# Loading x in 1 KB packets, with a column permutation on TensorE's output side

## The chip, the cores and the metric

One Trainium2 chip, one of its cores. The metric is the device time of the slowest core in microseconds (us); here there is one core, so it is that core's time.

## The reference

The kernel runs a cross attention between x (8 batches, 8 heads, 512 rows of 64) and a small state (32 rows per head), joins both read-outs to 544 rows of 512, applies a two-dimensional Fourier transform, and then a normalised two-layer MLP with a residual.

```python
scores  = x @ state^T / 8;   a  = softmax(scores);   xread = a  @ state   # 512 rows
scores2 = state @ x^T / 8;   a2 = softmax(scores2);  sread = a2 @ x       # 32 rows
X = concat(xread, sread)                     # (8, 544, 512) after joining the heads
u = X + real(fft(fft(X, axis=1), axis=2))
out = u + relu(layernorm(u) @ w_ch1) @ w_ch2 # w_ch1: 512 x 2048, w_ch2: 2048 x 512
```

## The kernel before

One row of x per partition; each packet of a load is one row of one head, 64 fp32 values, 256 B. The Fourier transform wants the 512 rows in an order in which rows 0 to 287 rise and the rest are mirrored. With one row per partition that order costs nothing: whole tiles are multiplied by an identity or by a mirror matrix and land in adjacent columns of PSUM.

```python
def load_x(b):                                  # six loads per batch, packets of 256 B
    xb = x[b].rearrange("h s d -> s h d")
    for n, (ps, si, rows) in enumerate(( (slice(32, 128), 2, xb[288:384]), (slice(0, 128), 0, xb[1:129]), ... )):
        queue = nc.scalar if b == 0 and n in (1, 3) else nc.sync
        queue.dma_start(out=xs[ps, si, :].rearrange("p (h d) -> p h d", d=D), in_=rows)

load_state(0, 1); load_x(0); load_state(1, 2); load_x(1)
nc.sync.dma_start(out=s_dram[2:]..., in_=state[2:, :, ::-1, :]...)   # states 2..7, first hop, to DRAM
load_state(2, B, s_dram)                                             # second hop, to SBUF

def more_loads():                               # GpSimd, in this order
    nc.gpsimd.tensor_copy(gate[:, 0:1], XQs[0][:, 3, 0, 0:1])
    cast_x(1); clears(1)
    nc.gpsimd.memset(stb[:, 2:]..., 0.0)

def last_loads():
    for hh in range(1, 4): low_tables(hh)       # reads the scratch that becomes the hidden layer's buffer
    nc.gpsimd.tensor_tensor(gate, xs_of[0][:, :, 0], w1[:, :, 3 * 512], op=ALU.add)   # waits for w1
    load_x(2)
    nc.gpsimd.tensor_copy(gate[:, 0:1], xs_of[2][:, 0, 0:1])                          # waits for x of batch 2
    for q in range(4): nc.gpsimd.dma_start(out=w2[:, q * 4:(q + 1) * 4, :], in_=...)  # fp32 read, bf16 written
    state_blocks(2, 3, nc.gpsimd.tensor_copy)   # waits for the states
    cast_x(2)

def turn_scores(g):                             # batches 2 to 7, two groups each
    p = qt("eTp")                               # a PSUM bank, 512 fp32 columns
    for si, o, rhs in ((0, 0, ident), (1, 128, ident), (2, 256, ident[:, 0:32]),
                       (2, 416, mirror[:, 0:96]), (3, 288, mirror)):
        nc.tensor.matmul(p[:, o:o + rhs.shape[1]], lhsT=E[:, si, g, :], rhs=rhs, start=True, stop=True)
    nc.scalar.activation(ET[:, g, :], p, AF.Copy, accum_out=sums[:, g:g + 1])
```

GpSimd works through its queue in order, so what stands behind a waiting instruction waits too. After `cast_x(2)` come the folds of batch 1 (tiles XE, XO, Sm), which VectorE (XQ) and then TensorE (gp) need. In the profiles ph and po are the matmuls of the MLP's first and second layer, gp and yp those of the transform, xT is x transposed, hT the hidden layer, eTp a group of scores, XR, XF and XL the read-outs, XE, XO and Sm GpSimd's folds.

The softmax here doesn't subtract the row's maximum and nothing guards it: scores larger than these inputs give would overflow.

## Time and profile before

| | before |
|---|---|
| time, median of 3 | 314.31 us (314.26 to 314.36) |
| span of the profiled run | 312.3 us |
| TensorE busy, 0 to 28.64 us (to the first MLP matmul) | 21.8 of 28.6 us |
| TensorE busy, 28.64 us to the end | 276.1 of 283.7 us |
| DMA packets, of them under 512 B | 114292, 105688 |
| a turned score group (5 matmuls, 512 columns) | 0.23 us |
| second hop of the states issued, used by GpSimd | 26.2 us, 35.8 us |

SyncE's wait for the first hop (engine and line, what was waited for, us, times, longest), and what GpSimd waited for before it could issue w1:

```profile
SPq L108 <- DMA s_dram<-in_state_dram: 14.1, 1, 14.1
10.14 0.19 POOL L274 COPY gate<-gen 128x4 f32<-128x4 f32 x1 [0.47 <-DVE gen L203]
```

A line in the order of time begins with its start and its length in us, then the engine, the line of the source and what is written and read; a bracket tells how long the engine had been idle and what ended it. In a chain of waits the columns are start, length, engine, tile and source line; "issue" there is time in which the profile shows nothing waited for.

### The profile page before, as it was taken

To read this page: it belongs to the slowest core of one execution; us is meant where nothing else is said; L and a number is where in the kernel's file an instruction comes from. 1 tells how busy PE (TensorE), PEld (TensorE's weight loads), DVE (VectorE), ACT (ScalarE), POOL (GpSimd) and SP (SyncE) were. 2 spreads that over 40 slices of the span, in tenths; PEclk is the share of its full clock that TensorE was granted. 3 is DMA by queue.
4 is the path that set the end of the run, shared out by engine and by line. 5 is a ranking of instruction groups with operands and counts; after the bars stand their busy time and mean duration, and the time that the engine had idled before them with its cause. 6 is when DMAs were issued, how large, how long until landed. Compare 5 with 4: busy or idle time off the path is not lost.

```text
span 312.3 us, 5918 instructions
## 1 busy us (share of the span) xinstructions
PE 297.9 (95%) x2268; PEld 171.3 (55%) x2300; DVE 184.9 (59%) x442; ACT 137.7 (44%) x269; POOL 74.8 (24%) x171
## 2 busy tenths in 40 slices
PE   5878999999999999999999999999999999999995
PEld 5666997544554545456645554455445544455443
DVE  8695882877778484864727774686559563100112
ACT  7698764635533543333542444234433432333300
POOL 8758884410240040300500024002200131000000
PEclk9999999999999999999999999999999999999999
DMA  9999999268354925268333684531333037303047
GB/s 158 187 200 180 173 181 186 59 113 180 61 109 85 201 65 136 67 129 160 80 80 78 144 177 95 126 84 52 80 75 68 34 76 99 79 36 67 34 105 166
DMA packets 114292, 34.86 MB, mean 112 GB/s; under 512 B 105688, under 2 KB 110040, under 8 KB 114264
## 3 DMA queue, kind: packets, MB, share of 16 engines
q1 hardware_dynamic: 103544, 28.72, 46.2%
q0 software_dynamic: 4224, 4.19, 8.6%
q10 hardware_dynamic: 6496, 1.57, 2.5%
q8 instruction: 18, 0.29, 0.4%
q14 instruction: 10, 0.08, 0.1%
HBM read 22.41 MB, written 14.02 MB: 117 GB/s over the span
## 4 chain that ended last, share of the span: by engine, by line
PE 79%; DVE 13%; ACT 2%; DMA 2%; issue 2%; SPq 0%; POOL 0%; DVEq 0%; POOLq 0%; ACTq 0%
PE po L768 32%; PE ph L703 29%; PE gp L578 4%; PE ph L713 3%; DMA xs<-in_x_dram 2%; DVE U L548 2%; DVE st L318 2%; PE po L760 1%; PE yp L544 1%; PE xfp L436 1%; PE xrp L436 1%; PE yp L543 1%; PE gp L582 1%; PE esp L411 1%; DVE XF L445 1%
## 5 line engine op out<-in xcount | busy, mean ns | idle before, releaser
L768 PE MATMUL po<-w,hT 128*128 128x512 bf16 x476 | 122.0, 379 | 1.5 <-issue 0.8
L705 ACT ACTIVATE hT<-ph 128x512 bf16<-128x512 f32 x112 | 66.9, 597 | 124.8 <-PE ph L703 124.8
L703 PE MATMUL ph<-unT,w 128*128 128x512 bf16 x437 | 114.0, 379 | 1.0 <-DVE ot L734 0.3
L703 PEld LDWEIGHTS <-w 128*128 128x128 bf16 x576 | 51.1, 98 | 47.9 <-issue 0.8
L768 PEld LDWEIGHTS <-hT 128*128 128x128 bf16 x496 | 47.1, 98 | 45.3
L734 DVE SCALAR_TENSOR_TENSOR ot<-po,rstd,U 128x512 f32<-128x512 f32 (+2 forms) x33 | 24.2, 732 | 52.8 <-PE po L768 44.9
L588 POOL COPY GL<-G 128x128 bf16<-128x128 bf16 x8 | 2.3, 291 | 113.6 <-ACT G L586 113.6
L548 DVE TENSOR_TENSOR U<-yp,XR 128x512 f32<-128x512 f32 x16 | 10.9, 683 | 27.0 <-PE yp L544 27.0
L318 DVE BATCH_NORM_STATS2 st<-U 128x6 f32<-128x512 f32 x32 | 21.8, 682 | 0.1
L324 POOL TENSOR_TENSOR rstd<-mv,epst 128x1 f32<-128x1 f32 x34 | 6.8, 200 | 62.9 <-DVE mv L320 62.9
L325 POOL TENSOR_TENSOR rstd<-rstd,mhalf 128x1 f32<-128x1 f32 x34 | 20.9, 615 | 2.7
L788 PE MATMUL warm<-ident 128*128 128x128 bf16 x152 | 13.5, 246 | 3.7 <-POOL ident masks.py:199 3.4
L586 ACT CAST G<-gp 128x288 bf16<-128x288 f32 x31 | 12.0, 397 | 10.7 <-PE gp L582 5.7
L713 PE MATMUL ph<-unT,w 128*128 128x128 bf16 x256 | 16.1, 219 | 0.5 <-ACT unT L624 0.5
L713 PEld LDWEIGHTS <-w 128*128 128x128 bf16 x256 | 15.0, 98 | 0.8 <-issue 0.6
L788 PEld LDWEIGHTS <-ident 128*128 128x128 bf16 x152 | 11.8, 113 | 4.7 <-POOL ident masks.py:199 3.4
L578 PEld LDWEIGHTS <-XQ 128*128 128x128 bf16 x96 | 8.8, 98 | 8.9 <-DVE XQ L508 2.6
L138 POOL CAST xin<-xs 128x2048 bf16<-128x2048 f32 x7 | 13.2, 1888 | 0.1
L612 DVE TENSOR_SCALAR ub<-U,mv 128x512 bf16<-128x512 f32 x24 | 12.3, 511 | 1.1 <-DVE mv L320 0.3
L436 PEld LDWEIGHTS <-ET 128*128 128x128 bf16 x80 | 7.0, 98 | 9.5 <-DVE XF L445 1.8
L445 DVE TENSOR_TENSOR XR<-xrp,rs 128x512 bf16<-128x512 f32 x16 | 11.1, 695 | 1.3 <-POOL XR L278 0.7
L715 ACT ACTIVATE hT<-ph 128x512 bf16<-128x512 f32 x16 | 9.4, 598 | 3.9 <-PE ph L713 3.9
(191 smaller groups left out, 350.4 us busy)
## 6 DMA issues: line engine op xcount, KB each, us to landing
xs<-in_x_dram SPq DMA_DIRECT2D x22, 256.0 KB, 5.0
w<-in_moe_w_ch_dram POOLq DMA_DIRECT2D x8, 512.0 KB, 10.4
out_dram<-ot SPq DMA_DIRECT2D x15, 256.0 KB, 2.5
r_dram<-ot SPq DMA_DIRECT2D x14, 256.0 KB, 2.0
out_dram<-r_dram SPq DMA_DIRECT2D x14, 256.0 KB, 3.6
xs<-in_x_dram SPq DMA_DIRECT2D x8, 192.0 KB, 4.5
xs<-in_x_dram ACTq DMA_DIRECT2D x2, 256.0 KB, 4.2
l_dram<-ot SPq DMA_DIRECT2D x2, 256.0 KB
```

The lines of the kernel that those rows point to most:

```text
L318: nc.vector.bn_stats(st6, u)
L325: nc.gpsimd.tensor_tensor(rstd, rstd, mhalf, op=ALU.pow)
L436: nc.tensor.matmul(ph[:, 0:260], lhsT=ET[:, g, c0:c0 + 128], rhs=rhs, start=True, stop=True)
L445: nc.vector.tensor_tensor(ov, in0=p[ps, :, 0:256].rearrange("p g (h d) -> p g h d", d=D), in1=rs[ps].unsqueeze(3).to_broadcast([n, 2, 4, D ...
L548: nc.vector.tensor_add(u.rearrange("p (k r) -> p k r", r=2), p.rearrange("p (r k) -> p k r", r=2)[:, 0:u.shape[1] // 2, :], x.rearrange("p ...
L578: nc.tensor.matmul(p[:, 0:NM], lhsT=XQ[:, j, c, :], rhs=tab[c], start=(c == 0), stop=(c == 2 and j != 2))
L703: nc.tensor.matmul(ph[:, o:o + n], lhsT=w1[:, c, f * 128:(f + 1) * 128], rhs=un_of[key][:, c, :], start=(c == 0), stop=(c == DC - 1))
L705: nc.scalar.activation(hT[:, per * i:per * i + per, :].rearrange("p a b -> p (a b)"), ph, AF.Relu, scale=-1.0 if key in flipped else 1.0)
L713: nc.tensor.matmul(ph[:, o:o + 128], lhsT=w1[:, c, f * 128:(f + 1) * 128], rhs=un_of[key][:, c, 128 * r:128 * r + 128], start=(c == 0), st ...
L734: nc.vector.scalar_tensor_tensor(ot[:, cols], in0=po_of[i][:, 0:cols.stop - cols.start], scalar=rstd, in1=u[:, cols], op0=ALU.mult, op1=AL ...
L768: nc.tensor.matmul(po_of[i], lhsT=h_of[key][:, f, i * 128:(i + 1) * 128], rhs=w2[:, f, :], start=(f == 0), stop=(f == FC - 1))
L788: nc.tensor.matmul(t[:, 0:128], lhsT=ident, rhs=ident, start=(i == 0), stop=(i == n - 1))
```

## The change

Its intent: fewer and larger packets for x, so that batch 0 lands sooner. Four consecutive rows of a head lie together in memory (1 KB), so a partition takes rows 4p to 4p + 3. The rows of x then lie four apart in the tiles, and the order that the transform needs is restored by the matmul that writes the scores: its output columns have a step of four. With it go fewer VectorE steps for the arguments of the sine tables, and a new order on several queues; the load of states 2 to 7 goes from behind batch 1's x to behind batch 2's.

```diff
     def load_x(b):
+        xb = x[b].rearrange("h (p i) d -> p h (i d)", i=4)
+        n = 2 if b == 0 else 4
+        for h in range(0, H, n):
+            queue.dma_start(out=xs[:, h:h + n, :], in_=xb[:, h:h + n, :])
     ...
-    nc.sync.dma_start(out=s_dram[2:]..., in_=state[2:, :, ::-1, :]...)
-    load_state(2, B, s_dram)
+    def load_more_state():                     # the same two hops, called later
     ...
-    state_blocks(0, 1)                         # ScalarE
-    nc.scalar.activation(CL..., zeros, AF.Copy)
-    nc.scalar.activation(SL..., zeros, AF.Copy)
+    state_blocks(0, 1, nc.gpsimd.tensor_copy)
-    nc.gpsimd.tensor_copy(gate, q2_[:, 0:4])   # GpSimd waited here for VectorE's second table
     for q in range(4): nc.gpsimd.dma_start(out=w1..., in_=...)
+    nc.gpsimd.memset(CL..., 0.0)
+    nc.gpsimd.memset(SL..., 0.0)
     clears(0)
+    state_blocks(1, 2, nc.gpsimd.tensor_copy)
     def more_loads():
         cast_x(1)
+        nc.gpsimd.tensor_tensor(gate, xs_of[0][:, 0:4, 0], w1[:, :, 3 * 512], op=ALU.add)
+        load_x(2)
+        load_more_state()
         clears(1)
         nc.gpsimd.memset(stb[:, 2:]..., 0.0)
     def last_loads():
-        nc.gpsimd.tensor_tensor(gate, xs_of[0][:, :, 0], w1[:, :, 3 * 512], op=ALU.add)
-        load_x(2)
     ...
     def scores_t(g):                           # batches 0 and 1: 4 matmuls become 18
-        for lo, hi, src in ((0, NM, slice(0, NM)), (NM, S, slice(S - 1, NM - 1, -1))):
+        for i in range(4):
+            x0 = 128 * i
+            for cols, rows in ((slice((i - 1) % 4, 285 if i == 0 else 288, 4), slice(x0 + (i == 0), x0 + 72)),
+                               (slice(287, 288), slice(0, 1)) if i == 0 else (None, None),
+                               (slice(291 - i, S, 4), slice(x0 + 127, x0 + 71, -1))):
     def turn_scores(g):                        # batches 2 to 7: 5 matmuls become 8
+            for si in range(4):
+                for o, rhs in (((3, ident[:, 1:72]), (287, mirror[:, 0:57])) if si == 0 else
+                               ((si - 1, ident[:, 0:72]), (291 - si, mirror[:, 1:57]))):
+                    nc.tensor.matmul(p[:, o:o + 4 * rhs.shape[1] - 3:4], lhsT=E[:, si, g, :], rhs=rhs, ...)
     ...                                        # cut: table arguments in fewer VectorE steps, constants, low rows
-    warm(48)
+    warm(12)
```

More of the change, by code (lines that the diff above doesn't have):

```diff
@@ L72 @@
     li = gen2[:, 3072:3072 + 384].bitcast(I32)
-    nc.gpsimd.iota(lt[:, 0:256], pattern=[[1, 256]], base=1, channel_multiplier=0)
-    nc.gpsimd.iota(lt[:, 256:NM], pattern=[[1, NL]], base=256, channel_multiplier=0)
+    nc.gpsimd.iota(lt, pattern=[[1, NM]], base=1, channel_multiplier=0)
     nc.gpsimd.iota(pi_[:, 0:2], pattern=[[128, 2]], base=1, channel_multiplier=1)
@@ L78 @@
     for hh in range(4):
-        nc.gpsimd.iota(pi_[32 * hh:32 * hh + 32, 2:3], pattern=[[0, 1]], base=256, channel_multiplier=1)
+        nc.gpsimd.iota(pi_[32 * hh:32 * hh + 32, 2:3], pattern=[[0, 1]], base=257, channel_multiplier=1)
     nc.gpsimd.iota(li[:, 0:128], pattern=[[2, 128]], base=1, channel_multiplier=0)
@@ L84, with more_constants @@
     mirror = singles.tile([128, 128], BF16, name="mirror")
-    nc.gpsimd.memset(halfpi, PI / 2)
-    nc.gpsimd.memset(mhalfpi, -PI / 2)
-    nc.gpsimd.memset(epst, eps)
-    nc.gpsimd.memset(mhalf, -0.5)
-    nc.gpsimd.memset(mirror, 0.0)
-    nc.gpsimd.affine_select(out=mirror, in_=mirror, compare_op=ALU.not_equal, fill=1.0, base=-127,
-                            pattern=[[1, 128]], channel_multiplier=1)
-    sg = singles.tile([128, 5], F32, name="sg")
-    nc.gpsimd.tensor_copy(sg[:, 0:1], pi_[:, 3:4])
-    nc.gpsimd.tensor_scalar(sg[:, 1:2], in0=sg[:, 0:1], scalar1=0.5, scalar2=-0.25, op0=ALU.mult, op1=ALU.add)
-    nc.gpsimd.tensor_scalar(sg[:, 1:2], in0=sg[:, 1:2], scalar1=float(1 << 23), scalar2=None, op0=ALU.add)
-    nc.gpsimd.tensor_scalar(sg[:, 1:2], in0=sg[:, 1:2], scalar1=float(1 << 23), scalar2=4.0, op0=ALU.subtract, op1=ALU.mult)
-    nc.gpsimd.tensor_scalar(sg[:, 0:1], in0=sg[:, 0:1], scalar1=-2.0, scalar2=1.0, op0=ALU.mult, op1=ALU.add)
-    nc.gpsimd.tensor_add(sg[:, 0:1], sg[:, 0:1], sg[:, 1:2])
-    turn_w = 2.0 * PI / 512 * (1.0 - 1e-6)
-    nc.gpsimd.tensor_scalar(sg[:, 2:3], in0=sg[:, 0:1], scalar1=PI / 2, scalar2=None, op0=ALU.mult)
-    nc.gpsimd.tensor_scalar(sg[:, 3:4], in0=sg[:, 0:1], scalar1=-turn_w, scalar2=None, op0=ALU.mult)
+    halves = ((halfpi, PI / 2), (mhalfpi, -PI / 2), (epst, eps), (mhalf, -0.5))
+    sg = singles.tile([128, 5], F32, name="sg")
+    sgi = singles.tile([128, 1], I32, name="sgi")
+    def more_constants():
+        for t, v in halves:
+            nc.gpsimd.memset(t, v)
+        nc.gpsimd.memset(mirror, 0.0)
+        for base in (-128, 0):
+            nc.gpsimd.affine_select(out=mirror, in_=mirror, compare_op=ALU.not_equal, fill=1.0, base=base,
+                                    pattern=[[1, 128]], channel_multiplier=1)
     stf = gen2[:, 1024:2048].rearrange("p (b g d) -> p b g d", b=B, g=2)
@@ L116, in load_x, with cast_x @@
     def load_x(b):
-        xs = wk.tile([128, 4, dm], F32, name="xs", tag="xs")
-        xb = x[b].rearrange("h s d -> s h d")
-        for n, (ps, si, rows) in enumerate((
-            (slice(32, 128), 2, xb[288:384]),
-            (slice(0, 128), 0, xb[1:129]),
-            (slice(0, 128), 1, xb[129:257]),
-            (slice(0, 128), 3, xb[384:512]),
-            (slice(2, 32), 2, xb[258:288]),
-            (slice(0, 2), 2, xb[0:258:257]),
-        )):
-            queue = nc.scalar if b == 0 and n in (1, 3) else nc.sync
-            queue.dma_start(out=xs[ps, si, :].rearrange("p (h d) -> p h d", d=D), in_=rows)
-        xs_of[b] = xs
-    def cast_x(b):
-        xs, t = xs_of[b], xin_bufs[b % 2]
-        if b == 0:
-            for si in (0, 3, 1):
-                nc.scalar.copy(t[:, si, 1:513], xs[:, si, :])
-            nc.gpsimd.tensor_copy(t[:, 2, 1:513], xs[:, 2, :])
-        else:
-            nc.gpsimd.tensor_copy(t[:, :, 1:513], xs)
+        xs = wk.tile([128, H, 4 * D], F32, name="xs", tag="xs")
+        xb = x[b].rearrange("h (p i) d -> p h (i d)", i=4)
+        n = 2 if b == 0 else 4
+        for h in range(0, H, n):
+            queue = nc.scalar if b == 0 and h in (0, 4) else nc.sync
+            queue.dma_start(out=xs[:, h:h + n, :], in_=xb[:, h:h + n, :])
+        xs_of[b] = xs
+    def cast_x(b, copy=nc.gpsimd.tensor_copy, lo=0, hi=H):
+        copy(xin_bufs[b % 2][:, :, 1 + D * lo:1 + D * hi].rearrange("p i (h d) -> p h i d", d=D),
+             xs_of[b][:, lo:hi, :].rearrange("p h (i d) -> p h i d", d=D))
     load_state(0, 1)
@@ L143 @@
     load_x(1)
-    nc.sync.dma_start(out=s_dram[2:].rearrange("b h j d -> (b h) j d"),
-                      in_=state[2:, :, ::-1, :].rearrange("b h j d -> (b h) j d"))
-    load_state(2, B, s_dram)
+    def load_more_state():
+        nc.sync.dma_start(out=s_dram[2:].rearrange("b h j d -> (b h) j d"),
+                          in_=state[2:, :, ::-1, :].rearrange("b h j d -> (b h) j d"))
+        load_state(2, B, s_dram)
     for i in range(2):
@@ L169 @@
     state_ones(0, 2)
-    state_blocks(0, 1)
+    state_blocks(0, 1, nc.gpsimd.tensor_copy)
+    more_constants()
     CL = singles.tile([128, 4, NM], BF16, name="CL")
     SL = singles.tile([128, 4, NM], BF16, name="SL")
-    zeros = gate2[:, 0:1].to_broadcast([128, 4 * NM])
-    nc.scalar.activation(CL.rearrange("p a b -> p (a b)"), zeros, AF.Copy)
-    nc.scalar.activation(SL.rearrange("p a b -> p (a b)"), zeros, AF.Copy)
-    cast_x(0)
+    cast_x(0, nc.scalar.copy, 0, 2)
+    cast_x(0, nc.scalar.copy, 2, 4)
+    cast_x(0, lo=4, hi=6)
     w1 = singles.tile([128, DC, dff], BF16, name="w1")
@@ L202, in absolute, with turn @@
     def absolute(q, f):
-        nc.vector.scalar_tensor_tensor(q, in0=f, scalar=-1.0, in1=f, op0=ALU.mult, op1=ALU.max)
-    def turn(W, N, lf, cols, scratch, eng=nc.vector):
+        nc.vector.tensor_scalar(q.bitcast(I32), in0=f.bitcast(I32), scalar1=0x7fffffff, scalar2=None, op0=ALU.bitwise_and)
+    def turn(W, N, lf, cols, scratch):
         n = len(cols)
-        f = scratch[:, 0:n * W].rearrange("p (n w) -> p n w", w=W)
-        q = scratch[:, n * W:2 * n * W].rearrange("p (n w) -> p n w", w=W)
+        f2d, q2d = scratch[:, 0:n * W], scratch[:, n * W:2 * n * W]
+        f, q = [t.rearrange("p (n w) -> p n w", w=W) for t in (f2d, q2d)]
@@ L209, in turn @@
         for i, c in enumerate(cols):
-            eng.tensor_scalar(f[:, i, :], in0=lf, scalar1=pf[:, c:c + 1], scalar2=None, op0=ALU.mult)
-        eng.tensor_scalar(q, in0=f, scalar1=1.0 / N, scalar2=float(1 << 23), op0=ALU.mult, op1=ALU.add)
-        eng.tensor_scalar(q, in0=q, scalar1=float(1 << 23), scalar2=-float(N), op0=ALU.subtract, op1=ALU.mult)
-        eng.tensor_add(f, f, q)
-        if eng is nc.vector:
-            absolute(q, f)
+            nc.vector.tensor_scalar(q[:, i, :], in0=lf, scalar1=pn[:, c:c + 1], scalar2=float(1 << 23), op0=ALU.mult, op1=ALU.add)
@@ L216, in turn @@
+        nc.vector.tensor_scalar(q2d, in0=q2d, scalar1=float(1 << 23), scalar2=-float(N), op0=ALU.subtract, op1=ALU.mult)
+        for i, c in enumerate(cols):
+            nc.vector.scalar_tensor_tensor(f[:, i, :], in0=lf, scalar=pf[:, c:c + 1], in1=q[:, i, :], op0=ALU.mult, op1=ALU.add)
+        absolute(q2d, f2d)
         return f, q
     shrink = 1.0 - 1e-6
-    nc.vector.memset(lt[:, 256:257], 0)
+    nc.vector.memset(lt[:, NM - 1:NM], 0)
     nc.vector.tensor_copy(pf, pi_)
-    for hh in range(4):
-        nc.vector.memset(pf[32 * hh:32 * hh + 1, 2:3], 0.0)
+    nc.vector.scalar_tensor_tensor(pf[:, 2:3], in0=pf[:, 2:3], scalar=float(NM), in1=pf[:, 2:3], op0=ALU.is_lt, op1=ALU.mult)
@@ L223 @@
+    pn = singles.tile([128, 3], F32, name="pn")
+    nc.vector.tensor_scalar(pn, in0=pf[:, 0:3], scalar1=1.0 / Stot, scalar2=None, op0=ALU.mult)
     f1, q1 = turn(NM, Stot, lt, [0, 1, 2], gen1)
-    f2 = gen2[:, 0:384]
-    q2_ = gen2[:, 512:896]
-    nc.vector.tensor_scalar(f2[:, 0:256], in0=li[:, 0:256], scalar1=pf[:, 3:4], scalar2=None, op0=ALU.mult)
-    nc.vector.tensor_scalar(f2[:, 256:384], in0=li[:, 256:384], scalar1=pf[:, 4:5], scalar2=None, op0=ALU.mult)
-    nc.vector.tensor_scalar(q2_, in0=f2, scalar1=1.0 / dm, scalar2=float(1 << 23), op0=ALU.mult, op1=ALU.add)
@@ L229 @@
-    nc.vector.tensor_scalar(q2_, in0=q2_, scalar1=float(1 << 23), scalar2=-float(dm), op0=ALU.subtract, op1=ALU.mult)
-    nc.vector.tensor_add(f2, f2, q2_)
-    absolute(q2_, f2)
+    fi = gen2[:, 0:384].bitcast(I32)
+    f2 = gen2[:, 384:768]
+    q2_ = gen2[:, 2048:2432]
+    nc.vector.tensor_scalar(fi[:, 0:256], in0=li[:, 0:256], scalar1=pf[:, 3:4], scalar2=None, op0=ALU.mult)
+    nc.vector.tensor_scalar(fi[:, 256:384], in0=li[:, 256:384], scalar1=pf[:, 4:5], scalar2=None, op0=ALU.mult)
+    turn_w = 2.0 * PI / dm * shrink
@@ new lines, in second_table @@
+    def second_table():
+        nc.vector.tensor_scalar(fi, in0=fi, scalar1=dm - 1, scalar2=None, op0=ALU.bitwise_and)
+        nc.vector.tensor_scalar(f2, in0=fi, scalar1=float(dm // 2), scalar2=None, op0=ALU.subtract)
+        absolute(q2_, f2)
+        nc.vector.tensor_scalar(sgi, in0=pi_[:, 3:4], scalar1=1, scalar2=None, op0=ALU.bitwise_and)
+        nc.vector.tensor_scalar(sg[:, 0:1], in0=sgi, scalar1=-2.0, scalar2=1.0, op0=ALU.mult, op1=ALU.add)
+        nc.vector.tensor_scalar(sg[:, 2:3], in0=sg[:, 0:1], scalar1=-PI / 2, scalar2=None, op0=ALU.mult)
+        nc.vector.tensor_scalar(sg[:, 3:4], in0=sg[:, 0:1], scalar1=turn_w, scalar2=None, op0=ALU.mult)
@@ L250, in more_sines @@
         w = 2.0 * PI / dm * shrink
-        nc.scalar.activation(TE[:, 0:128], q2_[:, 0:128], AF.Sin, bias=halfpi, scale=-w)
+        nc.scalar.activation(TE[:, 0:128], q2_[:, 0:128], AF.Sin, bias=mhalfpi, scale=w)
         nc.scalar.activation(TE[:, 128:256], q2_[:, 0:128], AF.Sin, bias=sg[:, 2:3], scale=sg[:, 3:4])
-        nc.scalar.activation(TO[:, 0:128], f2[:, 256:384], AF.Sin, bias=0.0, scale=-w)
+        nc.scalar.activation(TO[:, 0:128], f2[:, 256:384], AF.Sin, bias=0.0, scale=w)
         nc.scalar.activation(TO[:, 128:256], f2[:, 256:384], AF.Sin, bias=0.0, scale=sg[:, 3:4])
-        nc.scalar.activation(TE[:, 256:384], q2_[:, 128:256], AF.Sin, bias=halfpi, scale=-w)
+        nc.scalar.activation(TE[:, 256:384], q2_[:, 128:256], AF.Sin, bias=mhalfpi, scale=w)
         nc.scalar.activation(TE[:, 384:512], q2_[:, 128:256], AF.Sin, bias=sg[:, 2:3], scale=sg[:, 3:4])
-        nc.scalar.activation(TO[:, 256:384], f2[:, 128:256], AF.Sin, bias=0.0, scale=-w)
+        nc.scalar.activation(TO[:, 256:384], f2[:, 128:256], AF.Sin, bias=0.0, scale=w)
         nc.scalar.activation(TO[:, 384:512], f2[:, 128:256], AF.Sin, bias=0.0, scale=sg[:, 3:4])
@@ L284, in clears @@
         nc.gpsimd.memset(XNs[i].rearrange("p a b -> p (a b)"), 0.0)
-    nc.gpsimd.tensor_copy(gate[:, 0:1], xs_of[0][:, 3, 0:1])
+    nc.gpsimd.tensor_copy(gate, xs_of[0][:, 0:8:2, 0])
     for q in range(4):
         nc.gpsimd.dma_start(out=w1[:, :, q * 512:(q + 1) * 512], in_=w1v[:, :, q * 512:(q + 1) * 512])
+    nc.gpsimd.memset(CL.rearrange("p a b -> p (a b)").bitcast(F32), 0.0)
+    nc.gpsimd.memset(SL.rearrange("p a b -> p (a b)").bitcast(F32), 0.0)
     clears(0)
+    state_blocks(1, 2, nc.gpsimd.tensor_copy)
     def more_loads():
@@ L363, in turn_state @@
                 nc.tensor.transpose(p[:, pr * 128:(pr + 1) * 128], sb[:, g, 4 + 128 * hp:132 + 128 * hp], ident)
-            (nc.scalar.copy if b == 0 else nc.vector.tensor_copy)(sT, p[:, 0:512].rearrange("p (a b) -> p a b", b=128))
+            nc.scalar.copy(sT, p[:, 0:512].rearrange("p (a b) -> p a b", b=128))
+            cast_x(0, nc.scalar.copy, 6, 8)
         def turn_x(g):
             if b >= x_by_dma:
-                for si in ((0, 1), (3, 2))[g]:
+                for si in (2 * g, 2 * g + 1):
                     nc.sync.dma_start_transpose(out=xT[:, :, 128 * si:128 * si + 128], in_=xin[:, si, 1:513])
@@ L371, in turn_x @@
             p = qt("xTp", BF16)
-            for si in (0, 3, 1, 2):
-                for k in range(2):
+            for k in range(2):
+                for si in range(4):
                     o = k * 512 + si * 128
@@ L397, in scores_t @@
             p = qt("eTp")
-            for lo, hi, src in ((0, NM, slice(0, NM)), (NM, S, slice(S - 1, NM - 1, -1))):
-                for hp in range(2):
-                    nc.tensor.matmul(p[:, lo:hi], lhsT=sT[:, 2 * g + hp, :], rhs=xT[:, 2 * g + hp, src],
-                                     start=(hp == 0), stop=(hp == 1))
+            for i in range(4):
[3 more added lines that the diff above has]
+                                   (slice(291 - i, S, 4), slice(x0 + 127, x0 + 71, -1))):
+                    for hp in range(2 if cols else 0):
+                        nc.tensor.matmul(p[:, cols], lhsT=sT[:, 2 * g + hp, :], rhs=xT[:, 2 * g + hp, rows],
+                                         start=(hp == 0), stop=(hp == 1))
             nc.scalar.activation(ET[:, g, :], p, AF.Exp, scale=scale)
@@ L420, in turn_scores @@
             p = qt("eTp")
-            for si, o, rhs in ((0, 0, ident), (1, 128, ident), (2, 256, ident[:, 0:32]),
-                               (2, 416, mirror[:, 0:96]), (3, 288, mirror)):
-                nc.tensor.matmul(p[:, o:o + rhs.shape[1]], lhsT=E[:, si, g, :], rhs=rhs, start=True, stop=True)
+            for si in range(4):
+                for o, rhs in (((3, ident[:, 1:72]), (287, mirror[:, 0:57])) if si == 0 else
+                               ((si - 1, ident[:, 0:72]), (291 - si, mirror[:, 1:57]))):
+                    nc.tensor.matmul(p[:, o:o + 4 * rhs.shape[1] - 3:4], lhsT=E[:, si, g, :], rhs=rhs, start=True, stop=True)
             nc.scalar.activation(ET[:, g, :], p, AF.Copy, accum_out=sums[:, g:g + 1])
@@ L742, in store @@
                     nc.sync.dma_start(out=out[4 * dst + bq, 257:288, :].rearrange("r (c n) -> c r n", c=16),
-                                      in_=l_dram[dst, bq, 1:NL, :].rearrange("r (c n) -> c r n", c=16))
+                                      in_=l_dram[dst, bq, 0:NL - 1, :].rearrange("r (c n) -> c r n", c=16))
                 nc.sync.dma_start(out=out[4 * dst:4 * dst + 4, 0, :].rearrange("b (c n) -> c b n", c=16),
-                                  in_=l_dram[dst, :, 0, :].rearrange("b (c n) -> c b n", c=16))
+                                  in_=l_dram[dst, :, NL - 1, :].rearrange("b (c n) -> c b n", c=16))
             else:
@@ L796 @@
     t0 = transform(0)
-    weave((warmed(s0[:1], 4) + warmed(s0[1:3], 2) + s0[3:], 0, 1), ([lambda: state_blocks(1, 2, nc.vector.tensor_copy)], 0.7, 0.7))
+    for step in warmed(s0[:1], 4) + warmed(s0[1:3], 2) + [second_table] + s0[3:]:
+        step()
     weave((warmed(r0, 4), 0, 1), ([sines], 0.25, 0.25), ([more_sines], 0.3, 0.3), ([lambda: warm(44)], 1, 1))
```

## The prediction

> **What bounds the kernel now.** I first read the head of the page and the busy tenths, to see whether one engine fills the span.
>
> ```profile
> span 312.3 us, 5918 instructions
> PE 297.9 (95%) x2268; PEld 171.3 (55%) x2300; DVE 184.9 (59%) x442; ACT 137.7 (44%) x269; POOL 74.8 (24%) x171
> PE   5878999999999999999999999999999999999995
> DMA  9999999268354925268333684531333037303047
> ```
>
> The reader is to see two things. TensorE is full from the fifth slice (31 us) to the end, so there only fewer TensorE columns would shorten anything. The DMA engines are full in the first seven slices, which is where TensorE has its holes. I then cut the span at the first matmul of the first MLP layer (28.64 us) and at the first one of its second layer (49.73 us), in a table of windows with each engine's busy time.
>
> ```profile
> 0.00:28.64 28.64, 21.77 (x261) 18.53 (x262) 22.61 (x69) 22.68 (x48) 21.64 (x66) 1.00 1.09 178
> 28.64:49.73 21.09, 20.33 (x317) 18.70 (x317) 15.13 (x45) 15.67 (x31) 17.38 (x32) 1.00 1.21 173
> 49.73:312.30 262.57, 255.79 (x1691) 134.03 (x1721) 147.16 (x329) 99.38 (x192) 35.74 (x73) 1.00 0.47 99
> ```
>
> After 28.64 us TensorE idles for 0.8 + 6.8 us out of 284. Before it, its 21.8 us include 152 dummy warming matmuls (13.5 us of busy records), and no engine is really full: this is a chain of waits from the load of batch 0 to the first MLP matmul. In order of time the chain reads:
>
> ```profile
> 2.32 6.42 DMA xs<-in_x_dram
> ...
> 8.96 0.71 POOL xin L136
> 9.67 0.05 issue
> 9.72 0.30 PE xTp L375 x2
> 10.02 0.02 issue
> 10.04 1.02 ACT xT L376
> ```
>
> So batch 0 lands at 8.74 us, its last quarter is cast on GpSimd until 9.67, is transposed, and is copied until 11.06; the score matmuls begin at 11.11 and the exponentials end at 13.81. The next point is VectorE's first scaling of a read-out. In the waits and in the order of time it is held up by GpSimd:
>
> ```profile
> 10.39 0.19 POOL L288 COPY gate<-xs 128x1 f32<-128x1 f32 x1
> 10.76 3.26 POOL L290 DMA_DIRECT2D w<-in_moe_w_ch_dram  x4 [0.19 <-issue]
> ...
> 14.01 0.17 POOL L278 MEMSET XR<- 128x4 bf16 x1
> ...
> 14.21 0.70 DVE L445 TENSOR_TENSOR XR<-xrp,rs 128x512 bf16<-128x512 f32 x1 [0.69 <-POOL XR L278]
> ```
>
> GpSimd waits for batch 0 (its gate copy at 10.39), spends 3.26 us issuing the four w1 loads, and only then clears the border columns of XR, and VectorE waits 0.69 us for that. This second path, landing to gate to issue to clear, is as long as the first.
>
> **What the Trainium skill says.** (1) "DMA: Bandwidth & Descriptors", section "Why small descriptors are slow (HBM only)": a fixed overhead of about 3 cycles per packet, so 11 cycles instead of 8 for 256 B. The trace agrees that small packets are costly: in the queue list q1 moved 103544 packets of 277 B on average in 46.2% of 16 engines' 312.3 us, 22.3 ns each, and from 6 to 12 us the windows stay at 184 to 217 GB/s. (2) "TensorE: Matmul & The Clock Gate", section "Wait — 56ns, not 53.3ns?": warm start-to-start is N/2.4 GHz plus 2.5 ns, with a floor near 25 ns. The trace agrees: eight score matmuls of 64 columns, each with its own weights, start at 34.66 and the next group at 34.89, 29 ns each, so their weight loads are hidden. (3) The same page, "What's actually happening": TensorE is at half clock until a 3.4 us window was busy. Agrees: the 48 warming matmuls from 3.42 to 8.3 us take about 102 ns each, later ones 56 to 58. (4) "SBUF — State Buffer", section "SBUF: two separate sides": VectorE's two-input operations and GpSimd exclude each other. Agrees: two one-column GpSimd steps (L96, L97) took 1.05 and 1.02 us beside VectorE's two-input steps, and the next (L98) 0.19. For a matmul output with a stride in PSUM I found no page that gives a time.
>
> **The change part by part.**
>
> *x load.* Per batch 32768/8 = 4096 packets of 256 B become 1024 of 1 KB, in four loads (batch 0) or two instead of six. The packets of 4 x 256 B cost 4 x 22.3 = 89 ns; the w queue's packets (4.19 MB / 4224 = 993 B written, twice that read) cost 8.6% x 16 x 312.3 / 4224 = 102 ns, so a 1 KB packet without a cast should lie between 51 and 89 ns. I choose 65. Batch 0 then needs 1024 x 65 / 16 = 4.2 us instead of 4096 x 22.3 / 16 = 5.7, and lands at 8.74 - 1.5 = about 7.2, or 6.8 because the four issues are done some 1.5 us earlier. In the later batches the loads are hidden; their saving is worth nothing.
>
> *Score matmuls with a stride-4 output (batches 0 and 1).* Four matmuls of 288 and 224 columns per group become eighteen: two each of 71, 1, 56 and six each of 72, 56. By (2), per group 2 x (32 + 25 + 26) + 6 x (32.5 + 26) = 0.52 us against 4 x 2.5 + 1024/2.4 = 0.44 us. Four groups cost +0.3 us, half of it in batch 0, half in TensorE's full stretch.
>
> *Turning the scores (batches 2 to 7).* Five matmuls become eight, with 512 columns as before: about 8 x 2.5 + 213 = 0.23 us, against 0.23 in the chain now. Twelve groups: +0.1 us, +0.3 with some loss.
>
> *Table arguments, constants, clears.* VectorE's table steps run from 2.75 to 10.08 us now; they overlap with the wait for x, and VectorE then waits another 0.53 us for TensorE. Their saving (a 1.06 us absolute value becomes a 0.6 us step, a 1.06 us addition merges with the multiply) is therefore off the path. The state cast for batch 1 (1.38 us) leaves VectorE, the late part of the tables takes its place. GpSimd loses eight small steps (4.01 to 8.67 us). ScalarE loses both table clears (4.67 to 6.89 us) and so can cast x as it lands. But the two clears go to GpSimd, between the w1 issue and the clear of XR: 1584 columns take 1.41 us now, so 576 each are about 0.52, together +1.1 us on the second path.
>
> *The sum.* First path: land 6.8, last cast 7.4 (0.62), copy xT 8.4 (1.01), first score group 9.0, four exponentials of 0.54 with a wait between, XR possible at about 11.1. Second path: the GpSimd cast (0.70) and gate end at about 7.3; gate to clear took 14.18 - 10.39 = 3.8 us and takes 3.8 + 1.1 = 4.9 now, so XR starts at 12.2. **The second path is the longer.** Against 14.21 that saves 2.0 us. Behind it GpSimd has one more job (the state cast, 1.3 us) ahead of its folds, where it has about 0.5 us of room; I take 1.9. The rest of the chain to 28.64 and all of TensorE's stretch keeps its length and shifts. 314.3 - 1.9 + 0.3 = about **312.7 us**.
>
> **The rivals.** (a) *The whole 3 us of the first path arrive*, because GpSimd gets through sooner than I count. For: its queue loses more than 4 us of work. Against: landing, 3.26 us of issue and the added clears stay in its order. About 311.3 us, or 310.6 if x lands near 6.2. (b) *The strided output is slow.* If TensorE wrote a stride of 16 bytes at a quarter of the speed, each turned group would cost 0.64 us more, twelve 7.7 us, and the four score groups 5 us: about 324 us. Nothing in this trace tests it, since no output of the kernel before is strided; I think it unlikely[...]. (c) *TensorE stays cold longer*: 12 warming matmuls instead of 48 leave gaps before 8 us. The 40 or so matmuls to the first exponential would cost about 50 ns more each, some on the hidden part: +0.5 to +1.5 us, 313.2 to 314.2. (d) *The later state and w2 loads become a wait.* The re-ordered state now follows batch 2's x on the same queue, and its second hop waited 14.1 us for the first. The blocks are wanted by GpSimd at 35.8 us, and w2 by TensorE at 49.7, and both issues also move earlier: I expect nothing.
>
> **Range and chances.** The lower end, 310.6, is rival (a) in full; the upper end, 314.2, is rival (c), or losses of 0.1 us in each turned group. A gain over 2% would need 6.3 us, more than the whole time from the start to the landing can give. A loss over 2% needs rival (b). Hence 0.02 faster, 0.96 within 2%, 0.02 slower.
>
> **What would show it.** Landing of batch 0 between 6.2 and 7.4 us. The first scaling of XR at about 12.2 us, waiting for GpSimd's clear. The first MLP matmul at 26.5 to 27 instead of 28.64. The twelve turned groups at 0.23 to 0.28 us each. Windows after that first MLP matmul as long as now, within 0.7 us. The prediction is wrong if the strided groups take a multiple of that, if a DMA wait of TensorE appears after 28 us, or if the first scaling is released by something other than GpSimd's clear.

## The result

The changed kernel took 323.7 us (median of 3, 323.33 to 325.16) against 314.31: slower by 3.1%. Ratios here are the mean time of one kernel's runs over that of the other's of the same rounds (so not quite the ratio of the medians): 1.031, 95% interval 1.0261 to 1.036. Executions over 1.5% slower than the fastest of the same kernel are left out of the means. The result is correct. The time lies outside the predicted range, and the direction was wrong.

The head of the page, the busy tenths and the granted clock of the changed kernel:

```profile
span 321.9 us, 5985 instructions
PE 301.0 (94%) x2324; PEld 174.1 (54%) x2356; DVE 183.9 (57%) x440; ACT 135.4 (42%) x263; POOL 75.1 (23%) x172
PE   4988992999999999999999999999999999999995
PEclk9999998999999999999999999999999999999998
```

TensorE has a new hole in the seventh slice (48 to 56 us), after it had already been full, and in the same slice its clock falls. The chain of waits leads there:

```profile
29.58 2.98 POOL w L304 x4
32.56 14.12 issue
46.67 0.04 POOLq L121
46.72 0.25 POOL stb L144
...
48.03 1.95 POOL xin L121
...
53.62 0.57 DVE XQ L512
54.19 0.05 issue
54.24 1.62 PE gp L582 x6
```

Read it upwards. TensorE's gp waits for VectorE's XQ, that for GpSimd's folds, and those stand in GpSimd's queue behind the state blocks (stb), which start at 46.72. In front of them are 14.12 us called "issue". The list of waits (engine and tile, what was waited for, us, times, longest) names what it was, and the list of DMA issues gives its time from issue to landing in the last column:

```profile
POOL stb L144 <- DMA gen<-s_dram: 14.1, 1, 14.1
PE gp L582 <- DVE XQ L512: 5.6, 1, 5.6
```

```profile
s_dram<-in_state_dram SPq DMA_DIRECT2D x1, 384.0 KB, 5.1
gen<-s_dram SPq DMA_DIRECT2D x1, 384.0 KB, 14.9
```

It is the second hop of the states, issued at 31.8 us. Its 384 KB took 14.9 us; the first hop, with the same bytes, took 5.1. After the hole TensorE runs at half clock for a while. In this table of windows the columns after the stretch are its length, the busy time of five engines, the granted clock, the DMA share and GB/s:

```profile
52.00:54.00 2.00, 0.00 (x0) 0.00 (x0) 0.38 (x1) 0.00 (x0) 1.84 (x5) 0.97 0.59 120
54.00:56.00 2.00, 1.76 (x7) 1.04 (x8) 1.97 (x6) 0.50 (x2) 1.88 (x4) 0.50 0.45 92
56.00:58.00 2.00, 1.78 (x9) 1.00 (x9) 0.85 (x9) 0.30 (x1) 1.88 (x4) 0.68 0.77 47
58.00:60.00 2.00, 2.00 (x13) 1.07 (x12) 0.00 (x0) 0.80 (x2) 1.87 (x4) 1.00 0.82 256
```

The second find is the turned group itself. In the chains of waits of the kernel before and of the changed one, the same work, 512 columns:

```profile
61.44 0.23 PE eTp L423 x5
```

```profile
68.34 0.45 PE eTp L427 x8
```

With marks that both traces have, the 9.6 us between the two spans are accounted for:

| stretch | before, us | after, us | difference |
|---|---|---|---|
| start to batch 1's first gp matmul | 48.83 | 54.24 | +5.4 (5.8 of hole, 0.4 saved earlier) |
| from there to the first yp matmul | 4.43 | 5.92 | +1.5 (half clock) |
| from there to batch 2's last fold copy (GL) | 25.65 | 25.64 | 0.0 |
| from there to batch 7's, ten turned groups | 166.72 | 168.84 | +2.1 |
| from there to the end | 66.67 | 67.26 | +0.6 |

The intended part worked. From 4 to 8 us the DMA engines moved 323 to 358 GB/s (184 to 217 from 6 to 12 us before), packets fell to 89356, the last cast of batch 0's x on GpSimd ended at 8.2 us instead of 9.7, and batch 0's first gp matmul came 1.0 us earlier (20.23 against 21.27).

### The profile page after: what moved, and what is told of

Same layout as the page of the kernel before. It is cut to its first block, busy times and chain, and to the rows that moved or that the text cites. A ratio compares the mean times of both kernels' runs of the same rounds, so it can differ in the third digit from the quotient of the medians.

```text
span 321.9 us, 5985 instructions
## 1 busy us (share of the span) xinstructions
PE 301.0 (94%) x2324; PEld 174.1 (54%) x2356; DVE 183.9 (57%) x440; ACT 135.4 (42%) x263; POOL 75.1 (23%) x172
## 2 busy tenths in 40 slices
DMA packets 89356, 34.86 MB, mean 108 GB/s; under 512 B 72560, under 2 KB 85104, under 8 KB 89328
## 4 chain that ended last, share of the span: by engine, by line
PE 73%; DVE 10%; issue 6%; POOL 6%; ACT 3%; DMA 1%; DVEq 0%; POOLq 0%; ACTq 0%
PE po L772 31%; PE ph L707 29%; PE gp L582 3%; DVE U L552 2%; PE eTp L427 2%; DVE st L316 1%; PE po L764 1%; PE yp L547 1%; DMA gen<-in_state_dram 1%; POOL stb L144 1%; POOL xin L121 1%; PE yp L548 1%; POOL w L304 1%; PE xfp L440 1%; PE gp L586 1%
## 5 line engine op out<-in xcount | busy, mean ns | idle before, releaser
L590 ACT CAST G<-gp 128x288 bf16<-128x288 f32 x31 | 12.2, 397 | 17.7 <-PE gp L582 11.0
L121 POOL CAST xin<-xs 128x2048 bf16<-128x2048 f32 (+1 forms) x8 | 14.2, 1778 | 0.1
L792 PE MATMUL warm<-ident 128*128 128x128 bf16 x116 | 10.4, 236 | 3.6 <-POOL ident masks.py:199 3.3
L582 PE MATMUL gp<-CT,XQ 128*128 128x288 bf16 x32 | 7.1, 307 | 6.4 <-DVE XQ L512 6.4
```

Of the source, the lines that this page charges most:

```text
L121: copy(xin_bufs[b % 2][:, :, 1 + D * lo:1 + D * hi].rearrange("p i (h d) -> p h i d", d=D), xs_of[b][:, lo:hi, :].rearrange("p h (i d) -> ...
L582: nc.tensor.matmul(p[:, 0:NM], lhsT=XQ[:, j, c, :], rhs=tab[c], start=(c == 0), stop=(c == 2 and j != 2))
L590: nc.scalar.copy(G[:, j, :], p[:, 0:NM])
```

## The experiments

**Theory S.** The states' second hop, moved into the time of the w2 load, holds GpSimd, and through its folds TensorE, which then restarts at half clock. **Theory P.** A step of four columns in the matmul's output halves TensorE's rate. Rivals: the hole comes from another of the moves; the eight shorter matmuls with eight weight loads are slow in themselves (rival C); the second hop is slow whatever runs beside it.

### e1: the state load back in its old place

```diff
     load_x(1)
+    load_more_state()        # right after batch 1's x, as in the kernel before
     ...
         load_x(2)
-        load_more_state()
```

> The changed kernel with only the load of the later states (both hops) put back where the kernel before has it. Theory S (the late second hop, slowed by the w2 load, holds GpSimd for 14.1 us, and through its folds TensorE for 5.8 us and then at half clock for another 1.5): 323.7 - 7.3 = about 316.4 us, GpSimd's wait for the states gone, first gp matmul of batch 1 right after the 112 ph matmuls. Rival (the hole comes from the other moves, e.g. the GpSimd queue or the earlier x load): the hole moves to another wait and the time stays at 320 or above.

Measured: 316.75 us (316.26 to 317.48), correct, ratio to before 1.0074 (1.0057 to 1.0091). One moved call gives back some 7 us of the 9.4. Batch 1's gp starts at 49.05 us, straight behind the ph matmuls, and GpSimd no longer waits for the states (they are used at 33.6 us). From there to the first yp matmul it is 4.43 us again, at a clock of 1.00, so the half clock went with the hole. Theory S holds; the rival's hole at another place did not appear.

### e2: adjacent columns

```diff
-                    nc.tensor.matmul(p[:, o:o + 4 * rhs.shape[1] - 3:4], lhsT=E[:, si, g, :], rhs=rhs, ...)
+                    nc.tensor.matmul(p[:, o:o + rhs.shape[1]], lhsT=E[:, si, g, :], rhs=rhs, ...)   # other offsets o
```

> The changed kernel whose turned scores (batches 2 to 7) are written to adjacent PSUM columns by the same eight matmuls; the result is wrong on purpose. Theory P (a stride of four columns in the output halves TensorE's rate): each group falls from 0.45 to about 0.23 us, 12 x 0.22 = 2.6 us, so 321.1 us. Rival C (eight short matmuls with eight weight loads cost more than five): 323.7 us, groups stay at 0.45.

Measured: 322.59 us (320.81 to 323.15), ratio 1.0255 (1.0223 to 1.0287), wrong result (relative error 0.05). In the chain of waits the group is back to 0.24 us with the same eight matmuls:

```profile
69.17 0.24 PE eTp L427 x8
```

So the step is what costs. The whole time fell less than the 2.6 us expected. In the trace the five batches 3 to 7 are each 0.4 us shorter, 2.1 us for ten groups, while batch 2's groups show no gain: the stretch in which they lie is as long with the step as without it (the table's third row; 25.64 us in e2 too). And after the hole, which this kernel still has, the half clock lasted longer: from the first gp to the first yp matmul it took 6.57 us instead of 5.92.

### e3: the kernel before, with eight matmuls per group

```diff
-            for si, o, rhs in ((0, 0, ident), (1, 128, ident), (2, 256, ident[:, 0:32]), (2, 416, mirror[:, 0:96]), (3, 288, mirror)):
+            for si, o, rhs in ((0, 0, ident[:, 0:72]), (0, 72, ident[:, 72:128]), (1, 128, ident[:, 0:72]), (1, 200, ident[:, 72:128]),
+                               (2, 256, ident[:, 0:32]), (2, 416, mirror[:, 0:96]), (3, 288, mirror[:, 0:72]), (3, 360, mirror[:, 72:128])):
```

> The kernel before with its five matmuls per turned group cut into eight of 72, 56, 72, 56, 32, 96, 72, 56 columns, adjacent outputs, result right. Theory P: 314.3 to 314.6 us (8 instead of 5 times the 2.5 ns). Rival C: 314.3 + 2.6 = 316.9 us.

Measured: 313.99 us (313.88 to 314.11), correct, ratio 0.9991 (0.9976 to 1.0006): no loss. Rival C falls. (The 2.5 ns in the expectation are those of point (2) of the prediction.)

### e4: a sweep of steps

```diff
+            s, n = ((1, 64), (2, 64), ..., (8, 64), (1, 128), (2, 128), (3, 128), (4, 128))[2 * (b - 2) + g]
+            for si in range(4):
+                for c in range(0, 128, n):
+                    nc.tensor.matmul(p[:, 0:s * (n - 1) + 1:s], lhsT=E[:, si, g, :], rhs=ident[:, c:c + n], ...)
```

> Changed kernel, wrong on purpose: each turned group first writes 512 adjacent columns, then the same data again with a stride, one stride per batch and group: 1 to 8 with eight matmuls of 64 columns, then 1 to 4 with four of 128. Theory P, rate halves from some stride on: eight matmuls of 64 take 0.23 us at stride 1 and about 0.45 at stride 4; the runs of 128 columns show whether the loss is per column (0.22 to 0.43 us) or per matmul. If only multiples of four are slow, strides 3 and 5 stay at 0.23. Rival C: all alike. Time of the whole is not compared; about 326 us.

One look (325.69 us, state unknown, wrong result on purpose); only the groups are read. Group 1 of a batch comes before group 0, so of each pair of steps the second comes first in time. First the step of 8 with 64 columns, then steps of 2 and of 1 with 128; where the row that follows is shown, TensorE did not wait, and the difference of the starts is the time taken:

```profile
164.24 0.61 PE L431 MATMUL eTp<-ident,E 128*128 128x64 bf16 x8
164.66 1.05 PE L776 MATMUL po<-w,hTL 128*128 128x512 bf16 x4
...
198.82 0.60 PE L431 MATMUL eTp<-ident,E 128*128 128x128 bf16 x4
...
202.93 0.39 PE L431 MATMUL eTp<-ident,E 128*128 128x128 bf16 x4
203.15 1.03 PE L776 MATMUL po<-w,hT 128*128 128x512 bf16 x4
```

The step of 1 takes 203.15 - 202.93 = 0.22 us, the step of 8 takes 0.42. All of the steps 2 to 8 with 64 columns per matmul and 2 to 4 with 128 are alike, 0.40 to 0.42 us for 512 columns where nothing waited, odd steps as well as even. The loss is per column, a factor of two, and the size of the step, from 2 to 8, does not matter.

### e5: late states, but w2 after them

```diff
-        nc.gpsimd.tensor_copy(gate[:, 0:1], xs_of[2][:, 0, 0:1])
-        for q in range(4): nc.gpsimd.dma_start(out=w2..., in_=...)
         state_blocks(2, 3, nc.gpsimd.tensor_copy)
         cast_x(2)
+        for q in range(4): nc.gpsimd.dma_start(out=w2..., in_=...)
```

> The changed kernel with its late order of the state loads, but the state blocks and the cast of batch 2 stand ahead of the w2 loads on GpSimd, so w2 is issued only after the states have landed. Theory S with equal turns (a 256 B packet of the state takes turns with a w2 packet of about 102 ns on each DMA engine: 96 packets x 124 ns = 12 us): without w2 beside it the second hop takes 4 to 5 us instead of 14.9, GpSimd waits about 4 us instead of 14.1, no hole in TensorE: about 316.5 us. Rival (the second hop is slow by itself, small packets out of DRAM): still 14 us, 322 or more.

Measured: 318.12 us (three runs at 317.94 to 318.25, one at 322.15), correct, ratio 1.0165 (1.0098 to 1.0233). The second hop, now without w2 beside it:

```profile
gen<-s_dram SPq DMA_DIRECT2D x1, 384.0 KB, 3.8
```

3.8 us instead of 14.9 for the same transfer: it is not slow by itself, the w2 load beside it makes it so. GpSimd still waits 6.5 us for the states, not 4, but TensorE has no hole at 49 us. The time is 1.6 us above the expected one: TensorE waits 1.8 us for xT, the DMA transposes of batch 2, which now run beside w2 (that w2 delays them is argued, no run tests it). The slow fourth run was not profiled; its granted clock was 0.989, like that of the runs with the hole (0.988 to 0.995), where the other three had 0.997 to 1.0. Why it was slow is open.

### e6: the states ahead of batch 2's x

```diff
-        load_x(2)
         load_more_state()
+        load_x(2)
```

> The changed kernel, only the order on the SyncE queue exchanged: both hops of the states ahead of batch 2's x. The DMA engines are idle there (22 to 26 us in the changed kernel), so each hop takes about 4 us and the second is done by 33 us, before w2 starts. Theory S: about 316.5 us, like the first experiment. Rival: x of batch 2 comes some 5 us later and with it w2, and TensorE waits for w2 at 48 us: 318 or more.

Measured: 316.66 us (315.78 to 317.17), correct, ratio 1.0073 (1.0053 to 1.0093). The time is as expected, but the reason I wrote was not. In front of the gated x load nothing holds the states on the SyncE queue, so the hops were issued at about 4 and 11 us, not at 24. The second then ran beside the w1 load:

```profile
gen<-s_dram SPq DMA_DIRECT2D x1, 384.0 KB, 14.2
```

So another large GpSimd load slows it to the same 14 us (in e1, 14.5); here that is hidden, because the states are not wanted before about 33 us.

### e7: ScalarE puts the columns in order

All score matmuls of e6 write adjacent columns, and ScalarE, which copies PSUM to SBUF anyway, reads with a step in two instructions per group.

```diff
+        def sort_columns(g, p, how):
+            for h, (lo, hi) in enumerate(((0, 288), (288, S))):
+                v = p[:, lo:hi].rearrange("p (q k) -> p k q", q=4)
+                nc.scalar.activation(out=ET[:, g, lo:hi].rearrange("p (k q) -> p k q", q=4),
+                                     in_=v[:, :, ::-1] if h else v, **how(h))
```

> As e6_state_first, and all score matmuls (batches 0 to 7) write adjacent PSUM columns; ScalarE puts them in order while it copies (two instructions instead of one per group, reading with a step in PSUM). Result right. Theory P: 316.5 - 2.6 (turned groups) - 0.9 to 1.3 (score groups of batches 0 and 1, 0.92 us each now against 0.44 before) = 312.6 to 313.0 us, if ScalarE's second instruction (about 0.2 us each) stays off the path. Rival: reading PSUM with a step is as slow on ScalarE as writing it is on TensorE (0.6 to 1.2 us per group) and gives the gain back at the chain's start, 314 or more.

Measured: 315.08 us (6 runs, 313.98 to 316.14), correct, ratio 1.0024 (1.0001 to 1.0047). That is 1.6 us below e6, not 3.5 to 3.9. The rival about ScalarE's reading falls: its two copies with a step take 0.35 to 0.44 us each, 0.39 in the median, where the one without took 0.59, so about 0.2 us more per group, and each turned group needs a second read of its sum, another 0.2 us. The missing part is in two places. In batches 2 to 4 some 1.1 us is lost: from fold copy to fold copy, batches 3 and 4 take 27.11 and 37.34 us, against 26.64 and 37.14 before the change, and batch 2's stretch of the table 26.06 against 25.65. TensorE waits 0.35 us there for ScalarE's copy (at 62.6 us); the rest I did not trace. Batches 5 to 7 are as before the change within 0.01 us. The rest is early in the trace. The first MLP matmul starts at 26.37 us, 2.3 us earlier than before the change, but batch 1's gp only 0.6 us earlier. Between them ScalarE shows a wait that the kernel before does not have:

```profile
30.16 0.60 ACT L726 ACTIVATE hT<-ph 128x512 bf16<-128x512 f32 x1 [1.54 <-POOL SL L244]
```

### e8: which broken rows of columns are slow

```diff
+            o, rhs = ((p[:, 127::-1], ident), (pairs(p[:, 0:128])[:, :, ::-1], pairs(ident)),
+                      (fours(p[:, 0:256])[:, :, 0:2], pairs(ident)), (fours(p[:, 1:257])[:, :, 0:2], pairs(ident)), ...,
+                      (plain, xT[:, 0, 0:256:2]), (plain, xT[:, 0, 0:512:4]), ...)[2 * (b - 2) + g]
+            for si in range(4):
+                nc.tensor.matmul(o, lhsT=E[:, si, g, :], rhs=rhs, start=True, stop=True)
```

> Changed kernel, wrong on purpose: each turned group first writes 512 adjacent columns, then four matmuls of 128 columns with one pattern per group. If TensorE writes two adjacent columns at a time, runs of 2, 4 and 8 columns with gaps keep the full rate (0.22 us), runs of 2 that start at an odd column and reversed columns do not (0.43 us). If only a plain step of one is fast, all broken runs take 0.43. A step of 2 or 4, or reversed order, on the moving side: 0.22 us if the loss is one of the output alone.

One look (324.46 us, state unknown, wrong on purpose), again for the groups only, group 1 of a batch first. Runs of two with gaps from an odd column (first line) and from an even one (second); x on the moving side with a step of 4 (third) and of 2 (fourth):

```profile
91.58 0.60 PE L437 MATMUL eTp<-ident,E 128*128 128x128 bf16 x4
...
94.83 0.39 PE L437 MATMUL eTp<-ident,E 128*128 128x128 bf16 x4
...
197.55 0.62 PE L437 MATMUL eTp<-xT,E 128*128 128x128 bf16 x4
...
201.69 0.39 PE L437 MATMUL eTp<-xT,E 128*128 128x128 bf16 x4
```

A length of 0.39 belongs to the full rate (0.22 us from start to next start), 0.60 to the half rate. At the full rate: adjacent columns, also from an odd start; reversed columns; pairs swapped within themselves; runs of 2, 4 and 8 from an even column with gaps; reversed order on the moving side. At the half rate: a step of 2, and runs of 2 from an odd column. This is what pairs of columns at even addresses, written together, would give. That reversed columns would be slow, as I had written, was wrong. A step of 4 on the moving side (8 bytes) is slow too, one of 2 is not.

### e9 and e10: GpSimd's order

```diff
# e9, on top of e7's gathering: GpSimd clears while it is idle, fills the low tables, then waits for w1
-        nc.gpsimd.tensor_tensor(gate, xs_of[0][:, 0:4, 0], w1[:, :, 3 * 512], op=ALU.add)   # in more_loads
-        load_x(2); load_more_state(); clears(1); nc.gpsimd.memset(stb[:, 2:]..., 0.0)
+    def early_clears(): clears(1); nc.gpsimd.memset(stb[:, 2:]..., 0.0)                     # called before the transform
     def last_loads():
         for hh in range(1, 4): low_tables(hh)
+        nc.gpsimd.tensor_tensor(gate, xs_of[0][:, 0:4, 0], w1[:, :, 3 * 512], op=ALU.add)
+        load_more_state(); load_x(2)
# e10, on top of e9: the border columns of XF, XR and XL are cleared before w1 is issued
+    borders(0)
     nc.gpsimd.tensor_copy(gate, xs_of[0][:, 0:8:2, 0])
```

> e7_gather starts its first MLP matmul 2.3 us earlier than the kernel before but has only 0.6 us of that left at 48 us. Theory T: the buffer of the hidden layer is the scratch of the table arguments, so its first copy waits for GpSimd's low tables, and the change put the wait for w1, the clears of batch 1 and the clear of the state blocks ahead of them. Here GpSimd clears before that, fills the low tables, and only then waits for w1. If T holds, the wait of ScalarE's first hidden copy for GpSimd (1.5 us) goes and the time falls by about 1.5 us, to 313.6. Rival (w1 lands at 25 us and limits the stretch anyway, or the half clock of TensorE does): no change, 315.

Measured: 313.68 us (5 runs, 313.44 to 314.36), correct, ratio 0.9979 (0.9965 to 0.9992). The wait is gone, and the first hidden copy starts 1.6 us earlier:

```profile
28.52 0.62 ACT L728 ACTIVATE hT<-ph 128x512 bf16<-128x512 f32 x1
```

Theory T holds (e9 and e7 ran on different chips; against the kernel before on the same chip the step is from 1.0024 to 0.9979, the 1.4 us). This version and e10 are the only ones of the changed kernel that are below the kernel before, by 0.2%. In its trace batch 1's last fold copy comes at 50.92 us instead of 53.12. Of those 2.2 us, 1.1 are lost again by batch 7's, as in e7 all of it in batches 2 to 4, where ScalarE runs its longer copies, and 0.7 after it.

> As e9_tables_first, and GpSimd clears the border columns of XF, XR and XL before it issues w1, not 4.5 us after. In e7_gather the first scaling of XR starts at 12.0 us, released by that clear, while its matmul was done at about 10.7. Theory of my prediction (the clear behind the w1 issue is the path): XR starts at about 11.0 and everything follows 1 us earlier: e9 - 1.0. Rival: another wait takes its place at once (VectorE's second table, half clock), same as e9 within 0.3 us.

Measured: 313.84 us (313.72 to 314.43), correct, ratio 0.9985 (0.9972 to 0.9997): no gain over e9. The scaling of XR in e7 and in e10:

```profile
12.00 0.70 DVE L455 TENSOR_TENSOR XR<-xrp,rs 128x512 bf16<-128x512 f32 x1 [0.54 <-POOL XR L272]
```

```profile
11.84 0.69 DVE L462 TENSOR_TENSOR XR<-xrp,rs 128x512 bf16<-128x512 f32 x1
```

GpSimd's clear no longer holds it, but it starts only 0.2 us earlier. VectorE's second table ends at 11.56 there, so the rival was right: that work was next in line.

## Why the prediction was wrong

It put the time at 312.7 us with 0.96 on "within 2%". By its own steps:

- **The bound: right.** After the start only TensorE's own columns and TensorE's holes count. All of the loss but the 0.6 us in the tail is of these two kinds: a hole of 5.8 us with 1.5 us of half clock, and 2.1 us of slower columns.
- **The x load: right.** I estimated 65 ns for a 1 KB packet and a landing at 6.2 to 7.4 us. Batch 0 had landed by 7.3 to 7.6 us at the latest: its last two casts start then, on both engines, and none waits for a DMA. In e7, where ScalarE's last cast does wait for the load, it starts at 6.77. The DMA rate rose to 323 to 358 GB/s; only this comparison shows that the small packets were costly, the 22.3 ns of the prediction had nothing beside them.
- **The second path (landing, gate, issue, clear): right in e7, only nearly in the changed kernel.** I predicted XR's scaling at 12.2 us, released by GpSimd's clear; in e7 it is 12.00 and so released. In the changed kernel it started at 13.07: GpSimd's gate came at 8.12, not 7.3, since its four state casts (2.15 us) and the constants behind them kept it until 7.6, and VectorE's second table, which I had called off the path, ended at the same time as the clear (12.84 against 12.95). The gain at the start was 1.0 us, not 1.9. One reading was wrong from the outset: before the change GpSimd's gate at 10.39 did not wait for batch 0, which had landed by 8.96, when GpSimd's cast of it began. The copy in front of it waited 0.47 us for VectorE's table (the line shown before), so VectorE's tables were on this path, and the change removed that copy.
- **The score groups of batches 0 and 1: wrong, by the factor of two that follows.** I gave 0.52 us per group. Batch 1's took 0.92. Of the 1.0 us gained at the first MLP matmul 0.4 are left at the 112 ph matmuls, with batch 1's two groups between the two.
- **Rival (d), "I expect nothing": the step that failed and cost most.** This wait cost 6.9 of the 9.6 us. I saw that the state load moved and that its second hop had waited 14.1 us before. I took that wait for a property of its place in the queue, and did not ask what the first hop was running beside. It ran beside w1 (issued from 10.76 us, the hop at 11.26), as the second hop now runs beside w2. e1, e5 and e6 show that the neighbour decides: 14.9 us beside w2, 14.2 beside w1, 3.8 beside neither. From the counts: 384 KB are 1536 packets of 256 B, 96 on each of 16 engines. If each takes turns with one w packet of 102 ns (my estimate from the queue list before), 96 x (102 + 22) ns = 12 us, plus about 2 from issue to landing (a 64 KB store takes 2.1). The Trainium skill says it: "DMA: Bandwidth & Descriptors", section "Queues, rings and completion order", has each engine alternate between queues at packet granularity; the traces agree with 14.9 against 3.8 us. A packet there is a group of descriptors, typically 9 to 17; that it is the profile's packet, and that the turns go by one each, is an inference from these sums, not seen packet by packet.
- **Rival (b), the strided output: the right mechanism, thought unlikely.** I gave it 0.02, on a belief about TensorE's output that nothing in the trace tested, and 0.64 us per group. It is real with 0.22 us per group: a factor of two, not four. e2, e3, e4 and e8 settle it. The skill warns of it, which I overlooked (last section). The 324 us that I wrote for this rival agree with the measured time by chance; 6.9 of the 9.6 us have the other cause.
- **Rival (c), the cold start: seen, and hidden.** Eight of batch 0's transposes start over 0.85 us, 106 ns each, against 55 before. But the path led over GpSimd and VectorE. Where half clock did cost, at 54 us, I had not expected it. Of my signs of being wrong the group at a multiple of 0.23 us came (0.45); the DMA wait after 28 us came too, but at GpSimd, where I had not looked for it.
- **Not seen at all:** the move of the w1 wait ahead of the low tables. In the changed kernel it cost nothing, since w1 had landed when GpSimd asked (24.6 us). Once the states were early and took their turns from w1, it cost 1.5 us (e7 and e9).

**Open:** the 0.6 us in the tail, which is behind the last matmul and appears in every version with the new x order; the slow fourth run of e5; how ScalarE's longer copies cost e7 and e9 some 1.1 us in batches 2 to 4; and whether a load without a cast, or in small packets, would slow the second hop as w2 does.

## What to carry to other kernels

When a load is moved, look at what runs beside it in its new place and who stands behind its consumer in an in-order queue: here 384 KB in 256 B packets beside a large cast load took four times as long, and an unrelated fold waited for it. A permutation is not free because it hides in an access pattern: measure the pattern on the engine that carries it, and if that engine is the bound, try to give the permutation to one that is not (here that brought 1.6 us of the 3.5 to 3.9 expected). And a wait listed in the profile before the change (the 14.1 us of the first hop) is a sample of what such a transfer can do elsewhere.

## What the Trainium skill lacked or had wrong

- "PSUM — Partial Sum Buffer", section "Specifications (TRN2)", warns that any non-contiguous access pattern slows matmuls significantly, with cachelines of 8 bytes, but it gives no rate, and neither does "TensorE: Matmul & The Clock Gate". Here every step from 2 to 8 halved it (0.42 against 0.22 us per 512 columns). "Any" is too wide: runs of 2 fp32 columns from an even column with gaps, and reversed columns, kept the full rate (0.22 us).
- "SBUF — State Buffer", section "Specifications (TRN2)", asks for at least two hits in each line of 16 bytes for full bandwidth. On TensorE's moving side that did not do: a step of 4 bf16 elements, which leaves two in each line, took 0.44 us for 512 columns in e8, a step of 2 took 0.23 (one group each, in one look).
- "DMA: Bandwidth & Descriptors" states the turns between queues but not what they do to a load in small packets: 384 KB in 256 B packets took 14.9 and 14.2 us beside a GpSimd cast load, and 3.8 us without one.
